# Joining a new token order for the QUADW quads, two DMAs for the rows of maxima, a changed first spread, and wide unused products

## The chip, the cores and the metric

The kernel runs on one core of one Trainium2 chip. A core has TensorE (PE), VectorE (DVE), ScalarE (ACT), GpSimd (POOL) and a queue for DMA issues (SP); PEld in the profile is TensorE's weight load, which runs beside the matmuls. The metric is the device time of one launch in microseconds, lower is better. Everything is fp32 at the boundary, and the kernel gets its precision from products of "high" and "low" halves (fp32r operands and their remainders).

## The reference

One block of a conditioned transformer, with S = 2048 tokens and D = 576 channels:

```
sa, ca, ga, sb, cb, gb = split(silu(c) @ w_mod, 6)
h = layernorm(x) * (1 + ca) + sa
q = h @ wq          # 32 heads of 18
k = h @ wk          # one head of 18, shared
v = h @ wv          # one head of 18, shared
o = softmax(q k^T / sqrt(18)) v      # per head
x = x + ga * (o @ wo)
h = layernorm(x) * (1 + cb) + sb
x = x + gb * (gelu(h @ w1 + b1) @ w2 + b2)      # w1: 576 x 4608
```

## The kernel before

The tokens are cut in four blocks `tb` of 512 (TB), and a block in four tiles of 128 (NT). The work goes through three phases.

**Phase 1, projections.** The modulation is computed, `x` is normalised (`ln1_stats`, `ln1_apply`), transposed by TensorE and spread by `h_evac` (L226): ACT forms the modulated fp32 value `hf`, then DVE (`first=True`) or ACT copies its high half into `zt`, and the engine `e` subtracts to form the low half (L233). The weights are split likewise by `split_wq` (L380: ACT copies, POOL subtracts at L384) and `split_rest` (L386: one DVE subtraction on the last chunk's upper half). For the first block, a loop runs the five `h_evac`s with the subtraction on DVE and with the high half copied by DVE for even k. `busy(n)` (L390) issues n matmuls of 128x128 on the identity whose product nobody reads. `q_chunk`, `k_block` and `v_block` are the projection products; q goes through DRAM (`qscr`) and comes back with `load_q` as `QST[n]`, a tile per quad. At the end of the last block (`i == 4`) a `busy(1)`, one `unit()` and another `busy(1)` are issued; `unit()` computes row maxima of scores.

**Phase 2, attention.** The 32 heads by 4 blocks are 32 quads of 4 heads and 512 tokens: quad n has `tb, qd = divmod(n, 8)`. The softmax's row maximum is found one quad ahead from extra score products, negated, and written into two spare rows (high and low half) of each half of `QST[n + 1]`, so that the score product of the next quad comes out with it subtracted. What runs when in a quad is a string of tokens written out by hand: QUAD for n = 0 to 8, QUADW for n = 9 to 30, LAST for n = 31. The strings give the program order on TensorE, and with it the order in which each other engine gets its part, since every engine executes in order:

- `S0`, `S1`: a score matmul 64x128 by 512 into `psB` (L932) and ACT's exponential of it into `P` (L934); 64 a quad. The digit names the row group (64 of 128 rows) of TensorE that is used.
- `M0`, `M1`: a maxima matmul into `psM` (L319) and DVE's reduction of it (L954), for the next quad. `X1`: a matmul with a difference of keys into `psB` (L942) and ACT's relu (L945); `R1`: a maxima matmul into `psM` and a DVE operation that joins it with the relu's result (L952).
- `Vj`: j units of probability times V (`pv_mm`, L922), four matmuls each, into `psC`, which lag eight units behind the scores; a quad has 64.
- `F1`, `F2`: `smax_fin1` reduces the maxima on DVE; `smax_fin2` (L357 to L365) transposes them on TensorE into a bank of `psB`, lets ACT copy the high half (L359) and DVE form the low half (L360), and has SP issue four DMAs into the rows of `QST[n + 1]` (L364).
- `T1`, `RC`, `T2`, `OS`: the steps of `post_quad` (L731) for the quad before: after ACT's evacuation of `psC` (L738), which is issued when the last V unit of that quad is, DVE transposes (L741); `RC` is DVE's reciprocal (L744) and POOL's scaling (L745); `T2` transposes back (L747); `OS` has ACT copy the high half (L757), POOL subtract (L758) and SP issue four DMAs into `ATT[tb]`. The tile `ATT[0]` is made by a generator of later steps (L551), the others here, ahead of `OS`.
- `WO`: one piece of the output projection (`wo_next`, L723 and L727), only in QUADW and LAST.

`psB` has four banks and `psM` three. After every fourth V unit, `between` runs a step or two of two background generators: `fill` (weights of later steps, normalisation of finished rows by `ln2_rows`, L585 among it) and `prep` (sums of MLP weights on POOL with their DMAs). Four units are one key chunk; `prep` pauses at three "quiet" chunks whose numbers are computed from where `F2` and `RC` stand in the string (`kf`, `kr`, L989). SP issues all DMAs.

**Phase 3, MLP.** The MLP runs over 36 half steps `v` with products of sums of blocks (a Strassen-like scheme): the first layer's products at L1147, the gelu at L1156 to L1168 on ACT, DVE and POOL, sums of its results at L1226 and around it, the second layer's products at L1250. Beforehand `form` (L1061) makes sums of the activations on POOL. The bias `b2` times the gate is needed in `ln2_rows` and in the last rows: `load_b2` loads it into a tile of the pool `px` in attention, `b2_scaled` (L631, L632) multiplies it by the gate and by 2 on POOL. At the start of the MLP `B2["b"] = load_b2()` loads it once more, and at `v == 0` `b2_scaled` multiplies it once more.

The old string of QUADW, whose tokens the prediction names:

```
M1 M1 S0 S0 X1 S1 M0 V4 S1 M0 S1 S0 M1 M0 V4 M0 S1 S0 M0 S1 T1 M0 X1 V4 S1 RC S0 S0 M1 M0 S1 V4
S0 R1 M1 S0 S1 M0 S1 V3 S1 M0 S0 X1 M0 M0 S1 V2 M0 S1 S0 R1 V2 M0 X1 M0 S1 S0 S1 M0 V4 S0 T2 R1
M0 S1 OS S0 M1 WO S0 R1 M1 S0 M1 S0 X1 V3 S0 M1 M0 S1 S1 M1 S0 V3 M0 S1 S0 R1 S0 M0 X1 V3 M0 S1
X1 M0 S1 M0 S1 V4 S1 M0 R1 S0 M1 S0 V4 S0 M1 M0 F1 S1 S0 S1 V4 M0 S1 M0 X1 S0 M1 F2 V4 M1 S0 S0
S1 M0 S1 M0 V3 R1 S0 S0 S1 R1 M0 V3 S0 S1 M0 S1 M0 S1 V3 M0 S1 M1 S0 M1 S0 V3
```

The last V unit of the quad before is the eighth, so its evacuation (L738) comes after the second group, `V4 ... V4`, of a string.

Of the kernel before, what the change touches and what calls it, by code (L numbers as in the profile page):

```python
# [8 lines left out]
F32 = mybir.dt.float32  # L9
F32R = mybir.dt.float32r  # L10
AF = mybir.ActivationFunctionType
ALU = mybir.AluOpType
# [20 lines left out]
def block_kernel(ctx: ExitStack, tc, x, wqkv, wo, w1, b1, w2, b2, c, wmod, ident_in, out):  # L33
# [19 lines left out]
    def psB(): return PS["t"].tile([128, 512], F32, name="psB", bufs=PS["b"])  # L53
# [3 lines left out]
    def big(): return per.tile([128, 10, 512], F32R, name="big", bufs=3)  # L57
# [297 lines left out]
    def smax_fin2(n):  # L355
        p = psB()
        pe.transpose(p[:16, :128], MR.pop(n), ident)  # L357
        ms = pa.tile([16, 2, 128], F32R, name="ms")
        ac.activation(ms[:, 0], p[:16, :128], AF.Copy, scale=-1.0)  # L359
        ve.scalar_tensor_tensor(ms[:, 1], p[:16, :128], -1.0, ms[:, 0].bitcast(F32), op0=ALU.mult, op1=ALU.subtract)  # L360
        for g in range(2):
            for s in range(2):
                r = 64 * g + R3 + s
                sy.dma_start(QST[n][r:r + 1].rearrange("o p (t c) -> o (p t) c", c=128).bitcast(F32),  # L364
                             ms[8 * g:8 * (g + 1), s].bitcast(F32))  # L365


    for t in range(NT):
# [12 lines left out]
    def split_wq(k, cs):  # L381
        ac.activation(wqh[:, k, cs], wqr[:, k, cs], AF.Copy)
        if k < KD - 1:
            po.tensor_tensor(wql[:, k, cs], wqr[:, k, cs], wqh[:, k, cs].bitcast(F32), op=ALU.subtract)  # L384

    def split_rest(cs):  # L386
        o = wqh[64:, KD - 1, cs]
        ve.tensor_tensor(o, wqr[64:, KD - 1, cs], o.bitcast(F32), op=ALU.subtract)

    def busy(n):  # L390

        p = psB()
        for _ in range(n):
            pe.matmul(p[:, :128], ident, ident, start=True, stop=True)

    busy(6)
    for t in range(NT):
# [9 lines left out]
        mod_sum(k)  # L407
    mod_cols(0, psB(), sel)
    mod_cols(1, psB(), unity[:, :1])
    busy(5)  # L410
    for k in range(KD):
        split_wq(k, slice(504, WQC))
    split_wq(0, slice(0, 504))
    split_rest(slice(504, WQC))
    for k in range(KD):
        h_evac(hp[k], zt, k, ve, k % 2 == 0)
    for k in range(1, KD):
        split_wq(k, slice(0, 504))
    split_rest(slice(0, 504))
    pick = p1.tile([128, 2, 128], F32R, name="pick")  # L420
    ones = p1.tile([128, 1], F32, name="ones")
    ve.memset(pick.bitcast(F32), 0.0)
# [23 lines left out]
    for tb in range(NB):  # L446
        nz = big() if tb + 1 < NB else None
        for i, m in enumerate((4, 0, 1, 2, 3)):
# [15 lines left out]
            if tb == NB - 1:  # L464
                if i == 0:
                    unit()
                elif i == 3:
                    smax_fin1(0)
                if i == 4:
                    busy(1)  # L470
                    unit()
                    busy(1)
            if nz is not None:
                for k in {1: (0, 1, 2), 2: (3, 4)}.get(i, ()) if tb else {3: (0, 1, 2), 4: (3, 4)}.get(i, ()):
                    h_chunk(tb + 1, nz, k)
# [147 lines left out]
        yield  # L623

    def load_b2():
        b2g = px.tile([128, D], F32, name="b2g")
        sy.dma_start(b2g, b2.to_broadcast([128, D]))
        return b2g

    def b2_scaled(b2g):  # L630
        po.tensor_mul(b2g, b2g, BC[:, 2, :])  # L631
        po.tensor_scalar(b2g, b2g, 2.0, None, op0=ALU.mult)  # L632
        return b2g
# [99 lines left out]
    def post_quad(n, PV):  # L733
# [13 lines left out]
        ve.transpose(O, T.rearrange("p a b -> p (a b)"))  # L747
        yield
        if tb not in ATT:
            assert tb  # L750
            ATT[tb] = big()
        A = ATT[tb].rearrange("p (s k) t -> p s k t", s=2)
        if n == NQT - 1:
            os = A[:, :, KD - 1, :]
# [126 lines left out]


    LAG = 8
    QUAD = """S0 M0 S1 S1 M0 V3 S0 M1 S1 M0 M1 S0 V3 M0 S1 M1 S0 V2 M0 S1 S1 M0 X1 S0 V4 T1 X1 M0 M1 M0 S1 S0
            V4 S1 RC M0 S1 S0 M0 S0 M1 V3 S0 M1 R1 S1 S0 M0 X1 V3 M0 S1 S1 R1 S0 M0 S1 V3 M0 X1 M0 S0 S1 S0
            M1 V3 M0 S1 S1 M0 S0 R1 S0 V3 R1 S0 S1 M1 S0 M0 X1 V3 M0 S1 M0 S1 S0 S0 R1 V3 M0 X1 S0 M1 S0 M1
            V3 S1 M0 M0 S1 T2 S0 S1 V4 M0 S1 S0 M1 S0 M1 V3 S0 R1 S1 M0 F1 S1 S0 V3 X1 M0 S1 M0 R1 S0 F2 OS
            V4 M0 M1 S0 S1 M0 X1 V4 S1 M0 S1 S0 M1 M0 S1 V2 R1 S0 M1 S0 V2 S0 S1 M0 M1 V2 S1""".split()
    QUADW = """M1 M1 S0 S0 X1 S1 M0 V4 S1 M0 S1 S0 M1 M0 V4 M0 S1 S0 M0 S1 T1 M0 X1 V4 S1 RC S0 S0 M1 M0 S1 V4
            S0 R1 M1 S0 S1 M0 S1 V3 S1 M0 S0 X1 M0 M0 S1 V2 M0 S1 S0 R1 V2 M0 X1 M0 S1 S0 S1 M0 V4 S0 T2 R1  # L890
            M0 S1 OS S0 M1 WO S0 R1 M1 S0 M1 S0 X1 V3 S0 M1 M0 S1 S1 M1 S0 V3 M0 S1 S0 R1 S0 M0 X1 V3 M0 S1
            X1 M0 S1 M0 S1 V4 S1 M0 R1 S0 M1 S0 V4 S0 M1 M0 F1 S1 S0 S1 V4 M0 S1 M0 X1 S0 M1 F2 V4 M1 S0 S0
            S1 M0 S1 M0 V3 R1 S0 S0 S1 R1 M0 V3 S0 S1 M0 S1 M0 S1 V3 M0 S1 M1 S0 M1 S0 V3""".split()
# [88 lines left out]
    for n in range(NQT):  # L982
# [3 lines left out]
        else:  # L986
            order = LAST
        if n < NQT - 1:
            kf, kr = (sum(int(tok[1]) for tok in order[:order.index(a)] if tok[0] == "V") // 4 for a in ("F2", "RC"))  # L989
            quiet = kf - 2, kf - 1, kr - 1  # L990
        for tok in order:
            if tok[0] == "V":
# [357 lines left out]
    for v in range(NV):  # L1350
# [158 lines left out]
```

## Time and profile before

| what | value |
|---|---|
| median of 3 runs | 2224.63 us |
| lowest and highest of them | 2224.18 and 2224.81 us |
| the profiled execution: its own time | 2227.88 us |
| the profiled execution: its span in the trace | 2225.8 us |
| first score matmul of attention | 130.8 us |
| evacuations of the quads' outputs (L738), first and last | 176.4 and 1375.9 us |
| the MLP | from about 1390 us to the end |
| scores' exponentials on ACT (L934) | 2013 of 620 ns |
| maxima's reductions on DVE (L954) | 1476 of 682 ns |
| memory traffic | 308.00 MB, mean 138 GB/s |

A line of the trace's order of time reads: start in us, duration in us, engine, line, operation, written tile <- read tiles, size, count; in brackets the idle time of the engine ahead of it and what ended it. A row that stands for several instructions has their count behind an x and their whole stretch as its duration. A row of the busy time by stretches has the window and its length, then busy us and count of instructions for PE, PEld, DVE, ACT and POOL, then the granted clock of TensorE (1.00 is full), the DMA engines' share, and GB/s. A row of one line's instructions has the shortest, median and longest duration in ns, and the first and last start. The bottom line of the page's chain gives the share of each engine in the work that ended last.

### The profile page before, as it was taken

How to read it: one execution, taken by the hardware profiler on the slowest of the kernel's cores; microseconds unless marked ns; L12 is line 12 of the kernel's file. 1: busy time of each engine (PE TensorE's matmuls, PEld its weight loads, DVE VectorE, ACT ScalarE, POOL GpSimd, SP SyncE). 2: the span in 40 equal slices, each digit the busy share in tenths (PEclk: the TensorE clock that was granted, in tenths of full speed). 3: DMA queues.
4: the chain of work that ended last, by engine and by line, in shares of the span. 5: the costliest groups of instructions: out<-in, count | busy, mean ns of one | idle time of the engine just before them, and what ended most of it. 6: DMA issues, size and time to landing. Idle time of an engine off the chain costs nothing.

```text
span 2225.8 us, 46116 instructions
## 1 busy us (share of the span) xinstructions
PE 2204.6 (99%) x16638; PEld 1450.8 (65%) x16638; DVE 1931.1 (87%) x3417; ACT 1639.8 (74%) x3145; POOL 1524.9 (69%) x1761
## 2 busy tenths in 40 slices
PE   8999999999999999999999999999999999999999
PEld 6654545454544545445454446888888898989898
DVE  7589999999999999999999983887888878888887
ACT  5569999999999999999999998544444444343443
POOL 6654356666776687677676640988888867877776
PEclk9999999999999999999999999999999999999999
DMA  6242143343333332333333322666666646676664
GB/s 228 85 133 93 34 128 122 127 137 109 125 121 123 115 129 94 114 130 111 115 121 118 125 70 69 200 179 174 178 179 181 185 129 182 180 218 188 177 184 124
DMA packets 184776, 308.00 MB, mean 138 GB/s; under 512 B 19711, under 2 KB 75407, under 8 KB 184549
## 3 DMA queue, kind: packets, MB, share of 16 engines
q1 hardware_dynamic: 184405, 304.91, 44.2%
q8 instruction: 132, 2.16, 0.4%
q14 instruction: 95, 0.78, 0.1%
q10 hardware_dynamic: 144, 0.15, 0.0%
HBM read 200.97 MB, written 93.79 MB: 132 GB/s over the span
## 4 chain that ended last, share of the span: by engine, by line
PE 92%; ACT 1%; DVE 1%; POOL 0%; issue 0%; DMA 0%; ACTq 0%; POOLq 0%; DVEq 0%
PE psC L922 23%; PE psB L1147 18%; PE psA L1250 16%; PE psB L932 14%; PE psM L319 12%; PE psB L723 2%; PE psB L942 2%; PE psA L1284 1%; ACT P L934 1%; PE psA L723 0%; PE psB L155 0%; PE psB L248 0%; PE psB L357 0%; DVE mx L344 0%; DVE mx L337 0%
## 5 line engine op out<-in xcount | busy, mean ns | idle before, releaser
L934 ACT ACTIVATE P<-psB 128x512 f32<-128x512 f32 x2013 | 1055.0, 620 | 42.7 <-PE psM L319 19.4
L954 DVE TENSOR_REDUCE mx<-psM 128x1 f32<-128x512 f32 x1476 | 934.2, 682 | 30.7 <-PE psM L319 16.0
L932 PE MATMUL psB<-qst,KS 64*128 64x512 f32 x2013 | 606.3, 434 | 0.1
L319 PE MATMUL psM<-KS,qst 64*128 64x512 f32 x1722 | 591.5, 435 | 0.6 <-DVE mx L337 0.5
L922 PE MATMUL psC<-P,V 128*32 128x256 f32 (+3 forms) x6608 | 569.0, 440 | 0.0
L932 PEld LDWEIGHTS psB<-qst,KS 64*128 64x128 f32 x2013 | 302.6, 184 | 218.3 <-ACT P L934 185.5
L319 PEld LDWEIGHTS psM<-KS,qst 64*128 64x128 f32 x1722 | 284.0, 184 | 186.1 <-DVE mx L954 130.5
L1147 PE MATMUL psB<-ops,w1a 128*128 128x512 f32 x1512 | 393.8, 396 | 0.2 <-DVE h L1162 0.2
L1147 PEld LDWEIGHTS psB<-ops,w1a 128*128 128x128 f32 x1512 | 270.1, 188 | 46.6 <-DVE h L1162 0.6
L922 PEld LDWEIGHTS psC<-P,V 128*32 128x32 f32 x6608 | 147.0, 108 | 187.9 <-issue 160.4
L1256 DVE TENSOR_TENSOR XT<-psA,XT 128x576 f32<-128x576 f32 x330 | 241.7, 753 | 20.1 <-PE psA L1250 14.7
L1250 PEld LDWEIGHTS psA<-w2s,big 128*128 128x128 f32 x1584 | 222.9, 188 | 15.5 <-POOL big L1224 3.6
L1250 PE MATMUL psA<-w2s,big 128*128 128x288 f32 x1584 | 230.8, 295 | 0.9 <-POOL big L1224 0.8
L1160 ACT ACTIVATE psB<-gs 128x512 f32<-128x512 f32 x144 | 86.7, 602 | 127.9 <-DVE gs L1159 127.8
L1224 POOL TENSOR_TENSOR big<-s,big 128x512 fp32r<-128x512 f32 x132 | 170.9, 1295 | 10.6
L952 DVE CUSTOM_DVE_ANT_0 xc<-psM,xc 128x512 f32<-128x512 f32 x246 | 166.3, 682 | 12.7 <-PE psB L932 4.5
L1156 ACT ACTIVATE h<-psB,b1t 128x512 f32<-128x512 f32 x144 | 97.9, 680 | 102.0 <-PE psB L1147 79.7
L945 ACT ACTIVATE xc<-psB 128x512 f32<-128x512 f32 x246 | 154.6, 628 | 4.2 <-PE psM L319 1.5
L758 POOL TENSOR_TENSOR os<-O,os 128x512 fp32r<-128x512 f32 x31 | 39.9, 1286 | 171.3 <-ACT os L757 171.3
L1159 DVE SCALAR_TENSOR_TENSOR gs<-psB,h 128x512 f32<-128x512 f32 x144 | 98.5, 684 | 38.5 <-ACT psB L1157 38.3
L792 POOL TENSOR_TENSOR r<-r,r 128x256 fp32r<-128x256 f32 (+1 forms) x162 | 121.8, 752 | 13.0
L1165 ACT ACTIVATE big<-h 128x512 fp32r<-128x512 f32 x39 | 24.7, 633 | 133.8 <-DVE h L1162 133.8
(212 smaller groups left out, 3325.2 us busy)
## 6 DMA issues: line engine op xcount, KB each, us to landing
w1a<-w1scr SPq DMA_DIRECT2D x252, 256.0 KB
w2s<-w2sum SPq DMA_DIRECT2D x132, 288.0 KB
w1scr<-r SPq DMA_DIRECT2D x126, 256.0 KB
w2s<-w2scr SPq DMA_DIRECT2D x76, 288.0 KB
w2scr<-r SPq DMA_DIRECT2D x72, 288.0 KB
w2sum<-r SPq DMA_DIRECT2D x72, 288.0 KB
qst<-qscr SPq DMA_DIRECT2D x192, 72.0 KB
w1a<-w2scr SPq DMA_DIRECT2D x33, 288.0 KB
```

The source lines that it names most:

```text
L319: pe.matmul(o, QST[n][64 * g:64 * g + 64, p, 128 * qt:128 * (qt + 1)], KS[64 * g:64 * g + 64, 512 * kb:512 * (kb + 1)], start=True, stop=True)
L792: po.tensor_tensor(o[:, n:2 * n], src, o[:, :n].bitcast(F32), op=ALU.subtract)
L922: pe.matmul(PVt[n][32 * j:32 * (j + 1), cs], V[:, kc, :], t[:, j, cs], start=(kc == 0 and h0 == 0), stop=(kc == 15), skip_group_check=True)
L932: pe.matmul(t, KS[64 * g:64 * g + 64, 128 * kc:128 * (kc + 1)], QST[n][64 * g:64 * g + 64, i, :], start=True, stop=True)
L934: ac.activation(P[n, kc][:, 2 * i + g, :], t, AF.Exp, scale=SCALE)
L945: ac.activation(XC[-1], t, AF.Relu)
L952: ve.tensor_tensor_reduce(c, t, c, 1.0, -3.0e38, ALU.add, ALU.max, o)
L954: ve.tensor_reduce(o, t, axis=AX.X, op=ALU.max)
L1147: pe.matmul(o, x, y, start=(first and i == 0), stop=(i == len(terms) - 1), skip_group_check=True)
L1224: po.tensor_tensor(unit(u, 1), x, unit(u, 0).bitcast(F32), op=ALU.subtract)
L1250: pe.matmul(p[:, i, :288], x[:, ts_], W2S[k][:, y], start=(bool(first) and q == 0), stop=(q == 2), skip_group_check=True)
L1256: ve.tensor_tensor(o, p[:, :, :288], o, op=ALU.add)
```

## The change

It has five parts. (1) QUADW gets a new order of the same tokens; QUAD is wrapped anew, with its tokens as they were. (2) `smax_fin2` writes the rows of maxima with two DMAs instead of four, each covering both row groups. (3) In the first block's spread, `split_rest` gets its engine as an argument and runs once on POOL, ahead of `split_wq(0, ...)`; two of the five subtractions of `h_evac` (k = 1 and 3) go to POOL, and the high halves are copied by DVE for all k but 1. (4) `dense(n, w, x)` is added, n matmuls of the full 512 columns whose product nobody reads; a `dense(1)` replaces one of five `busy` products in the first block, and `dense(5)` and `dense(4)` replace the two `busy(1)` around the last `unit()`. (5) The scaled `b2` lives in the pool `per` and is kept, so that its second load and its second scaling go. Beside this, `post_quad` steps the generator `fill` until `ATT[0]` is there where it is wanted earlier, and the position of `F2` and `RC` reads V counts of two digits.

```diff
-        for g in range(2):
-            for s in range(2):
-                r = 64 * g + R3 + s
-                sy.dma_start(QST[n][r:r + 1].rearrange("o p (t c) -> o (p t) c", c=128).bitcast(F32),
-                             ms[8 * g:8 * (g + 1), s].bitcast(F32))
+        for s in range(2):
+            r = R3 + s
+            sy.dma_start(QST[n][r:r + 65:64].rearrange("g p (t c) -> g (p t) c", c=128).bitcast(F32),
+                         ms[:, s].bitcast(F32))
...
-    def split_rest(cs):
+    def split_rest(cs, e):
         o = wqh[64:, KD - 1, cs]
-        ve.tensor_tensor(o, wqr[64:, KD - 1, cs], o.bitcast(F32), op=ALU.subtract)
+        e.tensor_tensor(o, wqr[64:, KD - 1, cs], o.bitcast(F32), op=ALU.subtract)
...
+    def dense(n, w, x):
+
+        p = psB()
+        for _ in range(n):
+            pe.matmul(p, w, x, start=True, stop=True)
...
-    busy(5)
+    busy(2)
+    dense(1, ident, XT[:, 0, :512])
+    busy(2)
     for k in range(KD):
         split_wq(k, slice(504, WQC))
+    split_rest(slice(504, WQC), po)
     split_wq(0, slice(0, 504))
-    split_rest(slice(504, WQC))
     for k in range(KD):
-        h_evac(hp[k], zt, k, ve, k % 2 == 0)
+        h_evac(hp[k], zt, k, po if k in (1, 3) else ve, k != 1)
     for k in range(1, KD):
         split_wq(k, slice(0, 504))
-    split_rest(slice(0, 504))
+    split_rest(slice(0, 504), ve)
...
                 if i == 4:
-                    busy(1)
+                    dense(5, wqh[:, 0, :128], KS[:, :512])
                     unit()
-                    busy(1)
+                    dense(4, wqh[:, 0, :128], KS[:, :512])
...
     def load_b2():
-        b2g = px.tile([128, D], F32, name="b2g")
+        b2g = per.tile([128, D], F32, name="b2g")
...
         if tb not in ATT:
-            assert tb
-            ATT[tb] = big()
+            while not tb and tb not in ATT:
+                step(fill)
+            if tb not in ATT:
+                ATT[tb] = big()
...
+    QUADW = """M1 X1 S0 S1 M0 S0 R1 V4 M0 S1 M0 X1 S1 M0 V4 S0 M1 M0 S1 S0 S1 M0 V4 S0 M1 S0 S1 M0 X1 M0 V4 S0 M1
+            M0 S1 S0 S1 M0 V3 R1 S0 S1 R1 S0 M0 T1 S1 V4 S0 S1 M0 M1 M0 S1 V2 X1 S0 S1 M0 V3 RC M0 S1 S0 M1 S0
+            M1 V3 S1 S0 M0 M1 S0 S1 V3 M0 S1 S1 M0 S0 T2 R1 WO X1 M0 M1 M0 X1 S0 S1 V3 R1 S0 S0 M1 S1 M1 S0 V4
+            S0 M1 X1 M0 S1 S0 V3 R1 M0 S1 S0 S1 M0 V4 M0 S1 S0 R1 S0 S1 M0 V4 X1 F1 M0 S1 M0 M1 S0 F2 V3 S1 M0
+            S1 M0 S0 R1 S0 V3 M1 S0 M1 S0 S1 M0 S1 V3 M1 S0 S1 M0 M0 S1 OS V3""".split()
...
-            kf, kr = (sum(int(tok[1]) for tok in order[:order.index(a)] if tok[0] == "V") // 4 for a in ("F2", "RC"))
+            kf, kr = (sum(int(tok[1:]) for tok in order[:order.index(a)] if tok[0] == "V") // 4 for a in ("F2", "RC"))
...
-    B2["b"] = load_b2()
...
-        if v == 0:
-            b2_scaled(B2["b"])
```

More of the change, by code (lines that the diff above doesn't have):

```diff
@@ L883, in block_kernel @@
     LAG = 8
[L884 to L893, printed above, removed]
+    QUAD = """S0 M0 S1 S1 M0 V3 S0 M1 S1 M0 M1 S0 V3 M0 S1 M1 S0 V2 M0 S1 S1 M0 X1 S0 V4 T1 X1 M0 M1 M0 S1 S0 V4
+            S1 RC M0 S1 S0 M0 S0 M1 V3 S0 M1 R1 S1 S0 M0 X1 V3 M0 S1 S1 R1 S0 M0 S1 V3 M0 X1 M0 S0 S1 S0 M1 V3
+            M0 S1 S1 M0 S0 R1 S0 V3 R1 S0 S1 M1 S0 M0 X1 V3 M0 S1 M0 S1 S0 S0 R1 V3 M0 X1 S0 M1 S0 M1 V3 S1 M0
+            M0 S1 T2 S0 S1 V4 M0 S1 S0 M1 S0 M1 V3 S0 R1 S1 M0 F1 S1 S0 V3 X1 M0 S1 M0 R1 S0 F2 OS V4 M0 M1 S0
+            S1 M0 X1 V4 S1 M0 S1 S0 M1 M0 S1 V2 R1 S0 M1 S0 V2 S0 S1 M0 M1 V2 S1""".split()
+    QUADW = """M1 X1 S0 S1 M0 S0 R1 V4 M0 S1 M0 X1 S1 M0 V4 S0 M1 M0 S1 S0 S1 M0 V4 S0 M1 S0 S1 M0 X1 M0 V4 S0 M1
[3 more added lines that the diff above has]
+            S1 M0 S0 R1 S0 V3 M1 S0 M1 S0 S1 M0 S1 V3 M1 S0 S1 M0 M0 S1 OS V3""".split()
     LAST = """S1 S0 S1 S0 V8 S1 S0 T1 S1 S0 RC S1 S0 WO S0 S1 S0 T2 S1 V5 S1 S0 S1 S0 S1 OS S0 V11 S0 S1 S0 S1 S0
```

## The prediction

> **What bounds the kernel now.** I read the page first (busy shares, then the chain that ended last), then the busy time by stretches, then one quad in the order of time.
>
> ```profile
> span 2225.8 us, 46116 instructions
> ...
> PE 2204.6 (99%) x16638; PEld 1450.8 (65%) x16638; DVE 1931.1 (87%) x3417; ACT 1639.8 (74%) x3145; POOL 1524.9 (69%) x1761
> ...
> PE 92%; ACT 1%; DVE 1%; POOL 0%; issue 0%; DMA 0%; ACTq 0%; POOLq 0%; DVEq 0%
> ```
>
> The chain is TensorE's for 92% of the span; no other engine has more than 1%. An edit pays where PE waits, and nowhere else. In the attention stage the others are close behind (columns: span, then PE, PEld, DVE, ACT and POOL busy, clock, DMA share, GB/s):
>
> ```profile
> 600.00:800.00 200.00, 200.00 (x1757) 98.91 (x1753) 191.93 (x378) 189.92 (x383) 143.40 (x197) 1.00 0.34 113
> ```
>
> DVE is busy 191.93 and ACT 189.92 of 200 us, so neither has more than 5% to spare. The evacuation of a quad's output (L738) happens once a quad and marks the period; here it stands for a stretch of QUAD quads and then for one of QUADW quads:
>
> ```profile
> L738 ACT ACTIVATE O<-psC x7: 614/622/630, 214.2 to 439.2; 128x512 f32<-128x512 f32 x7
> ...
> L738 ACT ACTIVATE O<-psC x20: 597/597/601, 515.7 to 1266.9; 128x512 f32<-128x512 f32 x20
> ```
>
> That is 225.0/6 = 37.5 us for a QUAD quad and 751.2/19 = 39.5 us for a QUADW quad, which also does an output piece. QUADW drives 22 quads, n = 9 to 30. Inside one of them, PE's weight loads show bursts of score and maxima matmuls (S, M, X, R tokens) divided by groups of PV matmuls (V):
>
> ```profile
> 592.26 0.18 PEld L932 LDWEIGHTS psB<-qst,KS 64*128 64x128 f32 x1 [0.84 <-ACT P L934]
> ...
> 594.16 0.18 PEld L319 LDWEIGHTS psM<-KS,qst 64*128 64x128 f32 x1 [0.84 <-DVE mx L954]
> ...
> 596.26 0.40 PEld L932 LDWEIGHTS psB<-qst,KS 64*128 64x128 f32 x3 [0.84 <-ACT P L934]
> ...
> 596.96 0.18 PEld L932 LDWEIGHTS psB<-qst,KS 64*128 64x128 f32 x1 [0.18 <-ACT xc L945]
> ...
> 598.39 0.18 PEld L932 LDWEIGHTS psB<-qst,KS 64*128 64x128 f32 x1 [0.84 <-ACT P L934]
> ...
> 621.58 0.09 PEld L357 LDWEIGHTS psB<-ident,mxf 128*16 128x16 f32 x1 [0.37 <-ACT P L934]
> ...
> 622.78 0.18 PEld L319 LDWEIGHTS psM<-KS,qst 64*128 64x128 f32 x1 [0.84 <-DVE mx L954]
> ...
> 623.55 0.18 PEld L932 LDWEIGHTS psB<-qst,KS 64*128 64x128 f32 x1 [0.24 <-DVE ms L360]
> 624.76 0.18 PEld L319 LDWEIGHTS psM<-KS,qst 64*128 64x128 f32 x1 [0.62 <-DVE mx L954]
> ...
> 626.56 0.19 PEld L932 LDWEIGHTS psB<-qst,KS 64*128 64x128 f32 x2 [0.41 <-ACT P L934]
> ...
> 628.24 0.29 PEld L932 LDWEIGHTS psB<-qst,KS 64*128 64x128 f32 x2
> ```
>
> A burst starts at each of these rows except 596.96, 621.58 and 623.55. The waits of 0.6 to 0.84 us at their heads are the PV group streaming, not a stall. Six tokens and V4 take 592.26 to 594.16 = 1.90 us, seven tokens and V4 594.16 to 596.26 = 2.10, six and V3 626.56 to 628.24 = 1.68. Tokens of row groups 0 and 1 run in pairs, so six are three rounds and seven are four: a round costs 0.20, a V unit 0.22, and each burst about 0.4 beside them.
>
> **The quads' order.** Counting QUADW by this rule, old and new both have 69 rounds, 64 V units, 19 PV groups, one output piece and one F2 transpose. The PE work is the same, so the new order can win only what the old one loses in real waits and lose only what it adds. The old one's: the burst at 596.26 (T1 and the output's evacuation just ahead, three scores in its first three tokens) takes 2.13 instead of 1.90, lost 0.23, seen at 596.96; the burst at 624.76 takes 1.80 instead of 1.68, lost 0.12. Other bursts lose a few hundredths: about 0.4 us a quad, at most 0.4 x 22 = 8.8 to gain. The new order spreads its scores behind that evacuation evenly (S0 M1 S0 S1 M0 X1 M0), so I give it the 0.23. What it adds:
>
> - F1 and F2 now stand in one burst, followed by V3 instead of V4, so the next burst comes 0.2 us sooner, while DVE's copy of F2's result comes later behind F1. That copy frees a bank: 623.55 shows a score already held by it. I estimate 0.2.
> - OS moves to the end, so ACT's copy of the output stands ahead of the next quad's first exponentials, and four ACT tokens are due at once there: 0.1.
>
> Net -0.4 + 0.3, about -0.1 a quad; with a little off for the T2 wait below I take -1.5 us for 22 quads. Bounds: -8.8 (no wait left) and +6.6 (0.3 more a quad, the largest waits of these rows, 0.23 to 0.24, with a margin).
>
> T2 on DVE needs POOL's scaling of T (L745), which needs RC:
>
> ```profile
> 636.96 0.23 DVE L744 RECIPROCAL R<-T 128x16 f32<-128x16 f32 x1
> ...
> 640.80 1.05 POOL L745 TENSOR_TENSOR T<-T,R 128x512 f32<-128x512 f32 x1
> ...
> 646.15 0.66 DVE L747 STREAM_TRANSPOSE O<-T 128x512 f32<-128x512 f32 x1
> ...
> L585 POOL TENSOR_SCALAR Z<-XT,mv,rs x8: 2288/2294/2302, 546.0 to 1099.7; 128x576 f32<-128x576 f32 x8
> ```
>
> Here POOL starts 3.6 us after R ends and ends 4.3 us before T2. In the new order RC stands at V 28 and T2 in the burst at V 34, two bursts of 1.68 and most of a third, 4 to 5 us instead of 9. POOL may then be 3 to 4 us late. It is that late only where a normalised tile (L585, 8 of them) lies in its queue, and the output piece follows T2 at once and covers DVE. Value 0 to 0.1 a quad. QUAD is only wrapped anew, with the same tokens, and the wait for a missing ATT tile in post_quad concerns block 0 alone, which QUADW never handles before its tile is there: both cost nothing.
>
> **The two DMAs.**
>
> ```profile
> 622.97 2.82 SPq L364 DMA_DIRECT2D qst<-ms  x4
> ...
> 630.19 0.18 PEld L932 LDWEIGHTS psB<-qst,KS 64*128 64x128 f32 x1
> ```
>
> Four issues start at 622.97 over 2.82 us; the next quad's first score is at 630.19, without a wait. Two issues of the same bytes end 1.4 us sooner. In the new order that score comes some 7 us behind F2 instead of 8.6, still later. Value 0; no row shows the landing, so the bounds are 0 and -1.4 once, where attention begins.
>
> **b2 kept.** At the start of the MLP the b2 load and its two POOL products go.
>
> ```profile
> 1393.23 4.77 POOL L1061 TENSOR_TENSOR ops<-yr,ops 128x1024 fp32r<-128x1024 f32 x2 [40.32 <-ACT ops L1059]
> 1397.95 1.43 POOL L631 TENSOR_TENSOR b2g<-b2g,BC 128x576 f32<-128x576 f32 x1
> ...
> 1401.10 0.61 POOL L1167 CAST gt<-h 128x512 fp32r<-128x512 f32 x1
> ...
> 1407.01 0.30 PEld L1250 LDWEIGHTS psA<-w2s,big 128*128 128x128 f32 x2 [0.59 <-POOL big L1223]
> ...
> 1408.35 1.36 PEld L1250 LDWEIGHTS psA<-w2s,big 128*128 128x128 f32 x10 [1.04 <-POOL big L1224]
> ```
>
> POOL runs without a pause from 1393.23 to the operand that PE waits for at 1407.01 and 1408.35. PE's idle time there is 1.04 and, of the 0.59, about 0.4: 1.45 us. POOL comes 1401.10 - 1397.95 = 3.15 us sooner, more than that wait; behind it PE is late next itself. -1.45, bounds -3.15 and 0.
>
> **The dense products.** The clock falls to half three times:
>
> ```profile
> 18.20:21.60 3.40, 2.57 (x23) 2.38 (x23) 2.14 (x4) 2.33 (x5) 2.50 (x5) 1.00 1.06 389
> 21.60:25.00 3.40, 3.40 (x8) 2.37 (x9) 3.33 (x7) 3.37 (x7) 0.08 (x1) 0.50 1.05 392
> ...
> 48.90:52.30 3.40, 3.40 (x11) 1.80 (x10) 2.31 (x3) 3.37 (x6) 0.62 (x1) 0.50 0.79 266
> ...
> 130.80:134.30 3.50, 2.85 (x12) 1.33 (x11) 3.50 (x5) 2.51 (x5) 0.22 (x1) 0.99 0.57 157
> 134.30:141.10 6.80, 6.80 (x30) 2.84 (x32) 4.66 (x9) 4.71 (x9) 0.00 (x0) 0.50 0.94 294
> ```
>
> Each fall follows a stretch in which PE does little. dense(5) and dense(4) stand ahead of the third, in place of two small products:
>
> ```profile
> 123.01 2.36 PE L248 MATMUL psB<-big,wA 128*126 128x512 f32 x9
> ...
> 129.75 0.73 PE L319 MATMUL psA<-KS,qst 64*128 64x512 f32 x3 [0.63 <-DVE mx L337]
> ...
> 130.83 0.50 PE L932 MATMUL psB<-qst,KS 64*128 64x512 f32 x1
> 131.57 0.50 PE L319 MATMUL psM<-KS,qst 64*128 64x512 f32 x1 [0.24 <-DVE mx L337]
> ```
>
> One such product costs 2.36/9 = 0.26, so five cost 1.3 and four 1.05. The five lie in the wait for DVE that ends at 129.75; the four push the first score by 0.7 (129.75 + 0.73 + 1.05 = 131.53 against 130.83), but the maxima matmul at 131.57 waits for DVE anyway: cost 0.1. If the clock holds, 6.8 us at half rate become 3.4, less some 1.4 us in which the maxima are paced by DVE: -2.0, net -1.9. Bounds: -3.4 and +2.3 (all nine uncovered, clock falls all the same). [...]
>
> **The first spread.** split_rest and two of five subtractions go to POOL, one copy from ACT to DVE.
>
> ```profile
> 42.65 1.30 POOL L233 TENSOR_TENSOR big<-hf,big 128x512 fp32r<-128x512 f32 x1
> ...
> 42.96 1.54 DVE L233 TENSOR_TENSOR big<-hf,big 128x512 fp32r<-128x512 f32 x1 [3.00 <-ACT big L232]
> ...
> 50.66 0.69 DVE L233 TENSOR_TENSOR big<-hf,big 128x512 fp32r<-128x512 f32 x1 [0.59 <-ACT big L232]
> ```
>
> POOL needs 1.30 for what DVE does in 0.69, and beside it DVE's own took 1.54. DVE sheds work, but POOL's weight subtractions, next in the path, start later. Value 0; bounds -1.7 (half of the 3.4 us at half clock) and +1.2 (two subtractions, 0.61 dearer each). [...]
>
> **Sum.** -1.5 - 1.45 - 1.9 = -4.85. The profiled execution took 2227.88 us (span 2225.8), 3.25 above the median 2224.63; I set the change against the median: 2219.8.
>
> **Rivals.**
>
> - Nothing gained in the quads and the clock falls all the same: only b2 counts, 2223.2. [...] Against it: the visible 0.23.
> - No wait left in the quads: -8.8 - 1.45 - 1.9 = -12.15, 2212.5. For it: even spacing in most bursts. Against it: the banks held behind F2.
> - T2 waits for POOL (slower). POOL's queue at RC holds what the quad's start put there; if it is over 4 us late, DVE stalls at T2 and PE behind it. At 0.5 us in each of 22 quads, +11: 2224.63 + 11 - 3.35 = 2232.3. For it: the 3.6 us seen. Against it: the tiles lie in 8 quads, and the piece covers.
> - The change may not do what it says: dense may leave the clock as it is; that is in the first rival.
>
> **Chances.** Forecast 0.45, nothing 0.25, no wait left 0.18, T2 0.12. A measurement tells about 0.2% (4.4 us) from no change. Of the forecast's 0.45, at its edge, 0.29 is faster: faster 0.47, same 0.16 + 0.25 = 0.41, slower 0.12. The range leaves out most of T2's case and the ends: 2212 to 2228.
>
> **What would show it.** L738 in QUADW quads: 39.4 us a period is the forecast, 39.1 no waits, over 39.7 T2. No wait of PE on POOL at the first L1250. Full clock behind the first score. It is wrong if PE's period changes by more than 0.4 us, or if attention starts over 1 us later.

## The result and the profile after

The changed kernel takes 2243.25 us (median of 5 runs, 2241.53 to 2246.1) against 2224.63 us before on the same chip: 18.6 us slower, a ratio of 1.0085 with a 95% interval of 1.0073 to 1.0096. The forecast was 2219.8 us, the range 2212 to 2228.

Three lines of the page of the changed kernel come first: the span, the busy times, and the engines' shares of the chain that ended last.

```profile
span 2240.0 us, 46391 instructions
...
PE 2209.6 (99%) x16819; PEld 1456.6 (65%) x16819; DVE 1930.9 (86%) x3415; ACT 1642.5 (73%) x3144; POOL 1527.3 (68%) x1762
...
PE 84%; DVE 4%; POOL 4%; ACT 1%; issue 1%; DMA 0%; SPq 0%; POOLq 0%; DVEq 0%; ACTq 0%
```

No engine has more work to speak of, but the chain left TensorE: its share fell from 92% to 84%, and DVE and POOL, which had 1% and 0%, have 4% each. Something now ends last that involves both. The same evacuations as in the prediction show where (the lines of the new file are some seven to nine further down: L738 is L745, T2's L747 is L754):

```profile
L745 ACT ACTIVATE O<-psC x20: 597/624/657, 511.0 to 1282.5; 128x512 f32<-128x512 f32 x20
```

Nineteen periods of QUADW took 771.5 us, 40.6 us each, where they were 39.5; "over 39.7" was the prediction's mark for the wait at T2. From the evacuation that precedes them to the last one it is 920.0 us (471.4 to 1391.5) against 899.4 (476.5 to 1375.9): 20.7 us lost in the quads, so some 2 us seem to be won elsewhere. The instructions of T2's line name the cause (below the durations stands how long the engine was idle ahead of it, and how often):

```profile
L754 DVE STREAM_TRANSPOSE O<-T x32: 698/702/712, 192.9 to 1393.9; 128x512 f32<-128x512 f32 x32
...
its engine sat idle before it (us, times) until:
  POOL T L752: 11.3, 5
```

In the kernel before, this list was empty:

```profile
L747 DVE STREAM_TRANSPOSE O<-T x32: 656/702/712, 197.6 to 1378.3; 128x512 f32<-128x512 f32 x32
...
its engine sat idle before it (us, times) until:
who waited for it (us, times):
```

Now DVE stands still at T2 for 11.3 us, in five quads, until POOL has scaled T (L752). The longest of these waits, in the order of time, on POOL, DVE and TensorE's weight loads:

```profile
549.91 2.31 POOL L592 TENSOR_SCALAR Z<-XT,mv,rs 128x576 f32<-128x576 f32 x1
...
557.26 1.95 POOL L135 MEMSET qst<- 32x1024 f32 x2
...
569.36 0.79 POOL L840 TENSOR_TENSOR w2b<-w2b 128x288 f32<-128x288 f32 x1
570.11 1.05 POOL L752 TENSOR_TENSOR T<-T,R 128x512 f32<-128x512 f32 x1
```

```profile
562.63 0.24 DVE L751 RECIPROCAL R<-T 128x16 f32<-128x16 f32 x1
...
566.56 1.24 DVE L963 TENSOR_REDUCE mx<-psM 128x1 f32<-128x512 f32 x2
571.19 0.71 DVE L754 STREAM_TRANSPOSE O<-T 128x512 f32<-128x512 f32 x1 [3.39 <-POOL T L752]
571.83 0.65 DVE L961 CUSTOM_DVE_ANT_0 xc<-psM,xc 128x512 f32<-128x512 f32 x1
```

```profile
572.54 0.18 PEld L319 LDWEIGHTS psM<-KS,qst 64*128 64x128 f32 x1 [3.57 <-DVE mx L961]
```

None of these POOL rows has a bracket: POOL went from the normalised tile at 549.91 through the background steps without a pause, and reached the scaling at 570.11, 7.24 us after R was ready (562.63 + 0.24 = 562.87). T2 was due at about 567.8 and started at 571.19. Behind it on DVE stood R1's operation (L961), which holds a bank of `psM`; the maxima matmul that needs that bank waited 3.57 us, and with it everything on TensorE. The output piece covered nothing: it is a VectorE addition and products, and it stands behind R1 like the M tokens of the same burst.

The wait has a second price. The busy time by stretches, around that wait (columns as before; PEclk is the value behind the five engines):

```profile
569.00:572.50 3.50, 0.41 (x3) 0.00 (x0) 1.31 (x4) 0.60 (x1) 3.34 (x7) 1.00 0.25 87
573.70:577.10 3.40, 3.40 (x27) 1.59 (x22) 2.62 (x6) 2.73 (x7) 3.28 (x3) 0.50 0.47 176
```

TensorE did 0.41 us of work in 3.5 us, and then ran 3.4 us at half rate (0.50). The same followed one other of the five waits, that of 2.73 us. By an estimate from these lengths, two such stretches cost about 2 x 1.7 = 3.4 us. The three early ones that the kernel before showed (at 21.6, 48.9 and 134.3 us) are missing in this execution; what that is worth, the experiments say.

The periods of the quads, from the starts of these evacuations, give the rest of the account (us; in all rows but the first the background work also puts layer-norm statistics on DVE):

| evacuations starting at (after) | before | after |
|---|---|---|
| 1204 to 1283, little but sums in the background | 39.24 to 39.27 | 39.10 to 39.18 |
| every second quad, seven from 595 to 1084, in which DVE also copies transposed rows (`yr<-psB`) | 39.86 to 39.93 | 40.34 to 40.41 |
| between them, no wait at T2: 717 and 962 | 39.27 to 39.29 | 39.47 to 39.49 |
| between them, waits at T2: 551, 636, 797, 881, 1042 | 39.25 to 39.29 | 44.43, 40.99, 43.78, 40.69, 42.23 |

Against the 39.48 us of their neighbours without a wait, the five quads of the last row are 14.7 us longer together, which is the 11.3 us of waiting and the 3.4 us of the clock. The other 6 us of the 20.7 have nothing to do with T2: they are the 0.2 to 0.5 us a quad that the middle rows show.

### The profile page after: what moved, and what is told of

It is laid out like the page before. It is cut to its first block, busy times and chain, and to the rows that moved or that the text cites. A ratio compares the mean times of both kernels' runs of the same rounds, so it can differ in the third digit from the quotient of the medians.

```text
span 2240.0 us, 46391 instructions
## 1 busy us (share of the span) xinstructions
PE 2209.6 (99%) x16819; PEld 1456.6 (65%) x16819; DVE 1930.9 (86%) x3415; ACT 1642.5 (73%) x3144; POOL 1527.3 (68%) x1762
## 3 DMA queue, kind: packets, MB, share of 16 engines
q8 instruction: 133, 2.18, 0.4%
## 4 chain that ended last, share of the span: by engine, by line
PE 84%; DVE 4%; POOL 4%; ACT 1%; issue 1%; DMA 0%; SPq 0%; POOLq 0%; DVEq 0%; ACTq 0%
PE psC L931 20%; PE psB L1155 18%; PE psA L1258 16%; PE psM L319 11%; PE psB L941 11%; DVE mx L963 2%; PE psB L730 2%; PE psB L951 2%; PE psA L1292 1%; DVE xc L961 1%; POOL r L801 1%; PE psA L730 1%; ACT P L943 1%; POOL Z L592 0%; POOL r L800 0%
## 5 line engine op out<-in xcount | busy, mean ns | idle before, releaser
L941 PE MATMUL psB<-qst,KS 64*128 64x512 f32 x2013 | 591.3, 432 | 0.4 <-ACT xc L954 0.2
L931 PE MATMUL psC<-P,V 128*32 128x384 f32 (+3 forms) x6784 | 569.6, 433 | 0.0
L941 PEld LDWEIGHTS psB<-qst,KS 64*128 64x128 f32 x2013 | 308.2, 184 | 174.7 <-ACT P L943 125.1
L319 PEld LDWEIGHTS psM<-KS,qst 64*128 64x128 f32 x1722 | 271.1, 184 | 208.7 <-DVE mx L963 151.6
L931 PEld LDWEIGHTS psC<-P,V 128*32 128x32 f32 x6784 | 152.9, 108 | 194.9 <-issue 166.8
L767 POOL TENSOR_TENSOR os<-O,os 128x512 fp32r<-128x512 f32 x31 | 39.9, 1286 | 230.4 <-ACT os L766 219.2
L961 DVE CUSTOM_DVE_ANT_0 xc<-psM,xc 128x512 f32<-128x512 f32 x246 | 166.0, 681 | 19.7 <-PE psM L319 12.1
```

The source lines that it names most:

```text
L319: pe.matmul(o, QST[n][64 * g:64 * g + 64, p, 128 * qt:128 * (qt + 1)], KS[64 * g:64 * g + 64, 512 * kb:512 * (kb + 1)], start=True, stop=True)
L931: pe.matmul(PVt[n][32 * j:32 * (j + 1), cs], V[:, kc, :], t[:, j, cs], start=(kc == 0 and h0 == 0), stop=(kc == 15), skip_group_check=True)
L941: pe.matmul(t, KS[64 * g:64 * g + 64, 128 * kc:128 * (kc + 1)], QST[n][64 * g:64 * g + 64, i, :], start=True, stop=True)
L961: ve.tensor_tensor_reduce(c, t, c, 1.0, -3.0e38, ALU.add, ALU.max, o)
```

## The experiments

The theory after the traces was: the order alone costs the time, because T2 came closer to RC, POOL is not done with the scaling by then, and DVE stops. Rivals: the other parts carry some of the loss; DVE or POOL are overfull at that place whatever the distance; the gain that the first stage showed in the trace was real and hides a larger loss. Each run stands against the kernel before on the same chip (medians there 2224.0 to 2224.65).

**The order, without and alone.** The first kernel has the old QUADW in the changed file, the second the new QUADW in the file of before.

```diff
-    QUADW = """M1 X1 S0 S1 M0 S0 R1 V4 ...
+    QUADW = """M1 M1 S0 S0 X1 S1 M0 V4 ...
```

> The change with QUADW's old order put back; the rest of it stays. Theory (the order alone costs the time, because T2 on VectorE waits for GpSimd's scaling of T): attention still starts some 5 us earlier than in the kernel before (output evacuations of quad 0 at 171.7 instead of 176.4 us), the QUADW periods return to 39.26 and 39.9 us, no wait of VectorE at T2, and the b2 part stays: 2224.6 - 4.7 - 1.4 = 2218.5 us, 2216 to 2221. Rival (some of the loss comes from the other parts, by the moved DMAs, SP's queue or the kept b2): 2222 us or more.

Measured: 2224.4 us against 2224.0, ratio 1.0 (0.9992 to 1.0009). The quads are back at 39.26 and 39.9 us with no wait at T2, but the gain that the theory kept for the start did not appear in the median, so the 2216 to 2221 us were missed. The other four parts together neither gain nor lose, within the interval; what each does is told below.

> The kernel before with nothing but the new QUADW. Theory: the whole loss of the quads is here, + 20.7 us by the two traces, so 2245 us (2241 to 2249), with five or six quads in which VectorE stands 1 to 3.5 us at T2 for GpSimd. Rival (the order costs only together with the two DMAs or the kept tile): under 2235 us. The start of attention should stand as in the kernel before, 176 us for the first evacuation; if it comes at 172 to 174 us, the gain of the first stage was a matter of one execution and not of the change.

Measured: 2246.33 us, ratio 1.0098 (1.0084 to 1.0112), as the theory has it: waits at T2 of 3.43, 1.38, 2.73 and 2.65 us, and two of 0.3. Its first stage is that of the kernel before, and it tells what the comparison of two executions had hidden: the first evacuation starts at 172.6 us here, not at 176.4, with the same instructions. One wait of TensorE in the projections, from two executions of the same code, that of before and that of this kernel:

```profile
48.02 1.89 PEld L248 LDWEIGHTS psB<-big,wA 128*128 128x128 f32 x7 [2.90 <-ACT qs L279]
```

```profile
46.04 1.46 PEld L248 LDWEIGHTS psB<-big,wA 128*128 128x128 f32 x7 [1.40 <-ACT qs L279]
```

ACT waits there for a DMA that carries q to DRAM (`qscr<-qs`) to land, 2.18 us in the first of these executions and 0.69 in the second, so the landing differs by execution. Over the twelve traces TensorE's wait is 0.6 to 2.9 us, the longest in that of before; in that of the changed kernel it is 0.6. Against the 172.6 us of the second execution, 3.8 of the 4.7 us by which attention seemed to start earlier (171.7 against 176.4) are a matter of the execution and not of the change; the profiled execution of before lay 3.25 us above its median.

**Three ways to take the wait away.** They leave all work in. The first puts T2 later, the second leaves the tokens alone and moves POOL's background sums behind T2, the third puts RC earlier.

```diff
-... M0 S1 S1 M0 S0 T2 R1 WO ... S0 M1 X1 M0 S1 S0 V3
+... M0 S1 S1 M0 S0 R1 WO ... S0 M1 T2 X1 M0 S1 S0 V3
```

> The changed kernel with T2 moved from V 34 to V 41 of QUADW, so that it stands some 10 us behind RC, as in the old order; RC and everything else stay. Theory (T2 waits for the scaling): VectorE's waits at T2, 11.3 us in five quads, go, and the two half-rate stretches of 3.4 us that follow the longest two go with them (3.4 us): 2243.25 - 11.3 - 3.4 = 2228.5 us (2226 to 2232). Rival (VectorE or GpSimd are simply overfull at that place, and the wait moves to the next instruction that needs GpSimd): over 2238 us.

Measured: 2232.44 us, ratio 1.0036 (1.0023 to 1.0049). No wait at T2 is left, and no fall of the clock in the quads. But it is 4 us over the expected 2228.5: T2's 0.70 us on DVE now come into the burst at V 41, and the next one, at V 44, took 2.19 us instead of 1.89; so every quad pays 0.3.

```diff
+            early, late = ((kr - 3, kr - 2), (kr + 1, kr + 2)) if n > NQ else ((), ())
...
-        if n > 3 and kc not in quiet:
-            for _ in range(1 + (kc % 4 != 3)):
+        if n > 3 and kc not in quiet and kc not in early:
+            for _ in range((1 + (kc % 4 != 3)) * (1 + (kc in late))):
                 step(prep)
```

> The changed kernel with QUADW's order as it is; in quads 9 to 30 the background steps of GpSimd's weight sums that stood two and three chunks ahead of RC's chunk are issued behind T2 instead, the same number of them. Theory (what GpSimd has queued ahead of the scaling makes T2 wait): GpSimd has some 5 us less queued at RC, and of the five waits at T2, 1.1 to 3.4 us, at most small rests are left: 2243.25 - 11 - 3.4 = 2229 us, up to 2234. Rival (the wait is that of the short distance on VectorE itself, or GpSimd is overfull wherever the steps stand): 2238 us or more.

Measured: 2227.82 us, ratio 1.0018 (1.0009 to 1.0027). This is the cleanest of the three: in the quads, DVE and ACT have the changed kernel's instructions in the same order, and on POOL the scaling alone changes its place among the others. R and the scaling of the quad shown above, and the line of T2:

```profile
563.62 0.24 DVE L751 RECIPROCAL R<-T 128x16 f32<-128x16 f32 x1
...
564.97 1.42 POOL L838 TENSOR_TENSOR w2b<-w2b,BC 128x576 f32<-128x576 f32 x1
566.34 1.05 POOL L752 TENSOR_TENSOR T<-T,R 128x512 f32<-128x512 f32 x1
567.71 0.23 POOL L149 TENSOR_SCALAR rs<-mv 128x1 f32<-128x1 f32 x1 [0.32 <-DVE mv L148]
```

```profile
L754 DVE STREAM_TRANSPOSE O<-T x32: 698/701/711, 194.3 to 1379.9; 128x512 f32<-128x512 f32 x32
...
its engine sat idle before it (us, times) until:
who waited for it (us, times):
```

The scaling starts 2.48 us behind R (566.34 - 563.86) instead of 7.24, nothing stands under the idle time, and 15.4 us of the 18.6 are gone. What POOL had queued ahead of the scaling was the cause, and moving the queue alone removes it.

```diff
-... T1 S1 V4 S0 S1 M0 M1 M0 S1 V2 X1 S0 S1 M0 V3 RC M0 S1 ...
+... T1 S1 V4 RC S0 S1 M0 M1 M0 S1 V2 X1 S0 S1 M0 V3 M0 S1 ...
```

> The changed kernel with RC moved from V 28 to V 23 of QUADW, T2 and all else in place; the pause of the background sums moves with RC. RC comes 2.9 us earlier, and four of GpSimd's background steps, some 4 us, are no longer queued ahead of the scaling. Theory (T2 waits for what GpSimd has queued ahead of the scaling): all five waits at T2 (3.4 us the longest) go, and with them the clock's falls: 2243.25 - 11.3 - 3.4 = 2228.5 us, 2226 to 2232. Rival (the number of queued steps does not matter, only a fixed distance in V units): T2 is 11 V units behind RC then, not 6, and waits of 1 us or more remain in the quads with a normalised tile: 2233 us or more.

Measured: 2234.36 us, ratio 1.0044 (1.003 to 1.0058). All five waits are gone, so the rival of a fixed distance falls, though its time (2233 us or more) was met; the least margin between the scaling and T2 is 0.91 us. The time is again above the expected, and the quads with the least background work take 39.36 us instead of 39.12. The excess lies in the bursts behind the reciprocal's new place, V 25 (1.63 us instead of 1.45) and V 28 (1.79 instead of 1.72), so its 0.24 us on DVE probably came into a fuller stretch; no run tests this alone.

**What is left of the order.** With the wait gone by moved sums, the periods are 39.5 and 40.4 us where they were 39.27 and 39.9 before. By the starts of the bursts, three of them are longer in some of the quads with statistics than in those with the least background work: V 28 in the one half of the quads (2.07 us against 1.71), V 52 and V 61 in the other (2.16 against 1.88, 2.25 against 1.78). One more kernel moved the statistics a chunk earlier.

```diff
-        if kc % 2 and (held[0] != "T" or not pieces):
+        if (kc + (n > NQ)) % 2 and (held[0] != "T" or not pieces):
```

> The kernel with the background sums moved behind T2, and in quads 9 to 30 the steps of the other background work (finished rows' statistics on VectorE among them) called after even key chunks instead of odd ones, so one chunk earlier. Theory (the 0.2 to 0.5 us a quad that are left of the loss come from the two statistics of 0.45 us, which fall into the bursts with RC, F1 and OS): the bursts at V 28, V 52 and V 61 return to 1.72, 1.89 and 1.78 us from 2.07, 2.17 and 2.25, and the periods change by some tenths, to 39.1 to 39.3 and 39.7 to 40.0 if the new places have room: 2227.8 - 5 = 2223 us; 2220 to 2228. Rival (the excess belongs to the new tokens themselves): these bursts keep their times, 2227 to 2229 us.

Measured: 2229.94 us, ratio 1.0027 (1.0017 to 1.0037). Bursts, in us, medians over six or seven quads:

| burst | moved sums | and statistics a chunk earlier |
|---|---|---|
| V 25 | 1.45 | 1.73 |
| V 28 (RC) | 2.07 | 1.79 |
| V 31 | 1.68 | 2.10 |
| V 52 (F1, F2) | 2.16 | 2.20 |
| V 61 (OS) | 2.25 | 1.78 |

The excess leaves two of the three bursts and turns up in others, at or behind the ones where the statistics (0.45 us each on DVE) now fall, so it belongs to them and not to the tokens. The expected time was missed: the new places had no more room than the old ones. That V 52 kept its excess fits as well: in the trace, one statistic moved from the burst at V 48 to that at V 44, and the other (L147) from V 58, ahead of the excess at V 61, to V 52 itself.

**The start.** One kernel takes the first spread back, with the five small unused products ahead of it, and one the dense products; both have QUADW's old order.

```diff
+    split_rest(slice(504, WQC), ve)
-        h_evac(hp[k], zt, k, po if k in (1, 3) else ve, k != 1)
+        h_evac(hp[k], zt, k, ve, k % 2 == 0)
```

> QUADW's old order, and the first spread as in the kernel before (split_rest and all five subtractions on VectorE, five small unused products); the dense products, the two DMAs and the kept b2 stay. Theory (the new spread costs 1.0 us, because GpSimd's weight subtractions start later and TensorE waits for them): from the first projection product to the first key product 8.8 us instead of the 9.82 of the changed kernel, whatever the clock, and 2224.4 - 1 = 2223.4 us. Rival (the new spread is worth its trouble, because it removes a clock fall at 20 to 25 us): the stretch stays at 9.8 us or more, 2225 us or more.

Measured: 2222.31 us, ratio 0.9992 (0.9983 to 1.0001). The stretch from the first projection product to the first key product is 29.69 - 20.89 = 8.80 us, against 9.83 with the new spread. The waits that make it, first of the kernel with the new spread (the one with the old order), then of this one:

```profile
23.17 0.53 PEld L248 LDWEIGHTS psB<-big,wA 128*128 128x128 f32 x3 [0.61 <-POOL big L233]
...
25.99 2.62 PEld L248 LDWEIGHTS psB<-big,wA 128*128 128x128 f32 x12 [1.27 <-POOL big L233]
29.37 0.52 PEld L248 LDWEIGHTS psB<-big,wA 128*126 128x126 f32 x3 [0.76 <-POOL wA L383]
```

```profile
21.56 2.99 PEld L248 LDWEIGHTS psB<-big,wA 128*128 128x128 f32 x12 [0.38 <-DVE big L233]
25.05 1.92 PEld L248 LDWEIGHTS psB<-big,wA 128*128 128x128 f32 x9 [0.50 <-DVE big L233]
27.85 0.52 PEld L248 LDWEIGHTS psB<-big,wA 128*126 128x126 f32 x3 [0.88 <-POOL wA L383]
```

The two subtractions on POOL make TensorE wait 0.61 and 1.27 us. That costs 0.5 to 1.0 us: five executions with the old spread took 8.8 to 9.3 us for this stretch, all seven with the new one 9.81 to 9.83, also the one of them that had a half-rate stretch there. Four of the five with the old spread ran at half rate for 3.4 or 6.8 us at this place and the fifth, which did not, took 9.2 us, so the length of this stretch does not follow the clock.

By the durations, DVE and POOL also held each other up here: POOL's first subtraction took 1.75 us, where one of the same size took 1.30 in the prediction's row at 42.65, and two operations on DVE took about 1 us longer than in the old spread. The rows of the new spread (the kernel with the old order) come first, then those of the same copy and the same subtraction on DVE in the old spread:

```profile
21.37 1.75 POOL L233 TENSOR_TENSOR big<-hf,big 128x512 fp32r<-128x512 f32 x1 [0.40 <-ACT big L232]
24.55 1.39 POOL L233 TENSOR_TENSOR big<-hf,big 128x512 fp32r<-128x512 f32 x1 [1.43 <-DVE big L230]
...
21.99 1.42 DVE L230 CAST big<-hf 128x512 fp32r<-128x512 f32 x1
...
24.84 1.65 DVE L233 TENSOR_TENSOR big<-hf,big 128x512 fp32r<-128x512 f32 x1
```

```profile
22.02 0.42 DVE L230 CAST big<-hf 128x512 fp32r<-128x512 f32 x1
...
24.30 0.69 DVE L233 TENSOR_TENSOR big<-hf,big 128x512 fp32r<-128x512 f32 x1
```

Beside POOL's first subtraction a copy on DVE took 1.42 us instead of 0.42. POOL's second subtraction then waited 1.43 us for DVE's next copy, and beside it DVE's last subtraction took 1.65 us instead of 0.69. The one wide unused product that the new spread has ahead of it was not measured by itself.

```diff
-                    dense(5, wqh[:, 0, :128], KS[:, :512])
+                    busy(1)
                     unit()
-                    dense(4, wqh[:, 0, :128], KS[:, :512])
+                    busy(1)
```

> QUADW's old order, and the two small unused products in place of dense(5) and dense(4); all else as changed. Theory (the dense products keep the clock up at the start of attention and cost 0.7 us of a later first score): the clock falls to half for 3.4 to 6.8 us between 127 and 142 us; from the transposition of the first maxima to the first output evacuation 50.8 to 51.3 us instead of 49.5; 2224.4 + 1.5 = 2225.9 us. Rival (the fall was a matter of one execution): no fall there, 48.8 us for this stretch, 2223.7 us.

Measured: 2225.32 us, ratio 1.0005 (0.9996 to 1.0015). Without the dense products, and with them (the kernel of the old order), by stretches:

```profile
127.00:130.40 3.40, 2.62 (x11) 1.31 (x9) 2.80 (x4) 1.19 (x3) 1.28 (x1) 1.00 0.37 122
130.40:137.20 6.80, 6.69 (x24) 3.49 (x28) 6.52 (x11) 5.78 (x11) 0.00 (x0) 0.50 0.79 225
```

```profile
127.20:130.60 3.40, 3.40 (x15) 1.68 (x14) 2.80 (x3) 0.93 (x3) 1.29 (x1) 1.00 0.25 87
130.60:134.00 3.40, 2.59 (x12) 1.04 (x11) 3.40 (x7) 3.40 (x7) 0.00 (x0) 1.00 0.72 214
```

The theory of the dense products holds in size, with one limit. All three executions without them fell to half rate for 6.8 us there; of nine with them, six did not fall and three fell for 3.4 us. From the transposition of the first maxima to the first evacuation it is 50.5 to 51.2 us without, 49.2 to 49.5 with them and no fall, 50.2 to 50.6 with a fall. In the medians the two cannot be told apart (ratios to the kernel before of 1.0005 without them and 1.0 with them).

**Can the wait that the prediction saw be won back?** The prediction's gain in the quads was the burst at 596.26, 0.2 us longer than others like it. Two kernels (old order and old spread) rearranged it, so that its scores stand further apart.

```diff
-... T1 M0 X1 V4 S1 RC S0 S0 M1 M0 S1 V4
+... T1 M0 X1 V4 M1 S0 RC S1 M0 S0 S1 V4
```

> The old order with the old spread, the dense products, the two DMAs and the kept b2, and in QUADW one burst rearranged: S1 RC S0 S0 M1 M0 S1 behind the output's evacuation becomes M1 S0 RC S1 M0 S0 S1, so that its scores stand 2nd, 3rd, 5th and 6th among the tokens and not 1st, 2nd, 3rd and 6th. Theory (the 0.2 us that this burst is longer than others of six tokens and V4 is a wait for a bank that ScalarE holds while it evacuates the output, and can be won back): the burst takes 1.90 us instead of 2.11, 22 x 0.2 = 4.4 us: 2222.3 - 4.4 = 2218 us, the period 39.05 us. Rival (ScalarE or VectorE is full around it, so that the wait comes back in the bursts behind): the period stays at 39.27 us, 2222 us or more.

> As the other rearranged burst, but S1 RC M0 S0 M1 S0 S1: scores stand 1st, 3rd, 5th and 6th. Theory: the first score's bank is free in time, since the wait was seen at the second and third; 1.90 to 1.95 us for the burst, 2218 to 2219 us. Rival: the wait comes back in the bursts behind, period 39.27 us, 2222 us or more.

Measured: 2223.54 us, ratio 0.9995 (0.9986 to 1.0004), and 2222.7 us, 0.9992 (0.9983 to 1.0001), where 2218 was expected. The burst kept its 2.1 us, the period its 39.26. ACT in the second of them, around the output's evacuation (L743):

```profile
666.72 2.09 ACT L941 ACTIVATE P<-psB 128x512 f32<-128x512 f32 x4
668.75 0.60 ACT L743 ACTIVATE O<-psC 128x512 f32<-128x512 f32 x1
669.25 1.57 ACT L941 ACTIVATE P<-psB 128x512 f32<-128x512 f32 x3
670.68 0.63 ACT L952 ACTIVATE xc<-psB 128x512 f32<-128x512 f32 x1
671.21 4.17 ACT L941 ACTIVATE P<-psB 128x512 f32<-128x512 f32 x8
```

ACT has no pause for over 8 us around that wait. The reading is that the burst's scores wait for banks which ACT leaves only when it has worked off what lies before, and that the order of the scores in the burst changes nothing in that. Both runs fit it; none gives ACT less to do there.

No version is clearly faster than the kernel before. The best, the old order and the old spread with the dense products, the two DMAs and the kept b2, stands at 2222.31 us, 2.3 us below; its interval reaches 1.0001.

## Why the prediction was wrong, step by step

- **T2 behind RC: this is the step that failed.** The prediction saw the distance fall from 9 us to 4 or 5 (it was 4.9 in the quad shown), saw that POOL could be 3 to 4 us late, and still put 0 to 0.1 us on it, for two reasons. "It is that late only where a normalised tile ... lies in its queue" is true of the five waits, which all fall in quads with such a tile (five of the eight). But it took the lateness of the old place, 3.6 us in the quad shown and 4.15 at most, for that of the new one. RC stands 16 V units later there, so other background steps lie ahead of the scaling, and it came up to 7.24 us after R, with only 4.9 us to T2. And "the output piece follows T2 at once and covers DVE" left out R1 between them, whose bank TensorE needs at once. Measured: 11.3 us of waiting, 3.4 us of half rate behind it, and 15.4 us by the kernel that only moved the sums.
- **The bound of that term.** The end of +6.6 us for the quads came from waits of 0.24 us at other places, not from the queue of the engine for which the new wait would be. The rival had the mechanism, with 0.12 as its chance. That its 0.5 us in each of 22 quads is also the mean measured (11.3 / 22 = 0.51) is luck, since five quads had it all; its 2232.3 us lacked the clock's part and the statistics below.
- **The count of what is gained in the quads.** The forecast of -0.1 us a quad was measured at -0.13 where the background has little to do (39.26 to 39.13), and the equal counts of rounds were right. But its sum does not follow from its own terms: it grants the new order 0.23 us and then subtracts 0.4, and 0.23 against the 0.3 that is added would have been a loss of 0.07. That the size came out is partly luck. By the bursts' lengths in these quads, the burst at V 12 still takes 2.1 us (2.14 us where it was 2.12) but holds seven tokens instead of six, so one round of 0.2 now fits into what was a wait. OS costs 0.1 as forecast (V 61, 1.78 us against 1.68 for six tokens and V3). F1 and F2 in one burst cost the forecast 0.2 (1.88 against 1.68), but the old F2's burst already lost as much (2.10 against 1.90), which the prediction did not count.
- **The background's own steps on DVE** were left out, a term that the prediction put at nothing, though its window from 600 to 800 us had DVE at 96%. Where statistics fall on DVE the quads lose 0.2 to 0.5 us. By the kernel with moved sums this is about 5 us (904.5 us for the stretch of quads against 899.4).
- **The two DMAs:** 0, as forecast. SP issues them in 1.70 us instead of 3.26 ahead of the first score, and the first score comes 5.64 us behind the transposition without the dense products, 5.68 before.
- **b2 kept:** forecast -1.45. From the last evacuation to the end it is 849.9 us before and 850.1 with the order alone. In the kernels that keep b2 it is 848.4 to 848.6 with the new order, so -1.5 to -1.7, and 848.9 to 849.4 with the old one, so -0.5 to -1.0. No wait for POOL is left at the first product of the second layer.
- **The dense products:** forecast -1.9, measured -1.0 to -2.1 between the transposition and the first evacuation when the clock holds, and about -0.5 when it falls all the same, which happened in 3 of 9. The price was 0.7 us and not 0.1: the first score comes 6.4 us behind the transposition instead of 5.7, and no later wait swallows that; the measured gain has it in already. What sets these three apart from the six without a fall, no run shows.
- **The first spread:** forecast 0, bounds -1.7 and +1.2; measured +0.5 to +1.0, by POOL's subtractions being late. The upper bound counts POOL's 0.61 a subtraction and nothing for DVE, but DVE's last subtraction took 1.65 us beside POOL's instead of 0.69, much like the 1.54 in the prediction's row at 42.96. What TensorE waits for is POOL's two results, 0.61 and 1.27 us, the second of them late by DVE's copies too. The fall of the clock on which the bound of -1.7 counts cost nothing, since the stretch takes as long without it (9.2 us, against 8.8 to 9.3 with it).
- **What was set against the median.** The stretches at half rate in the profiled execution of before were taken as the median's. That execution was 3.25 us slower than the median, with a wait at 48 us that was 1.5 us longer than in the other trace of the same first stage. Its fall at 48.9 us is in none of the other eleven traces. A gain read from it was partly no gain.

## What to carry to other kernels

When two dependent steps on one engine are moved closer together with a step on another engine between them, price the other engine's queue at the new place, counting every background instruction that stands ahead there, and ask which bank the next instruction behind the waiting one holds. In this stage, where DVE is busy for 96%, half a microsecond found no free place: T2's 0.70 us cost 0.3 in a new burst, the reciprocal's 0.24 us cost about as much as it takes, and the statistics of 0.45 us cost 0.2 to 0.5 a quad where the new order met them. Before a short wait of TensorE is counted as a gain, look whether the engine it waits for has a pause around it; here ACT had none for 8 us, and two rearrangements of the burst won nothing.

## What the runs showed of the hardware

- Some of the waits at T2 within the quads were followed by half rate on TensorE (a granted clock of 0.50): 3.4 us of it after the waits of 3.39 and 2.73 us in the changed kernel, and 6.8 and 3.4 us after those of 3.43 and 2.65 in the kernel with the order alone. TensorE itself stood still for 2.4 to 3.2 us each time. The waits of 1.1 to 1.4 us were not followed by it, and neither were the 2.65 us of the changed kernel and the 2.73 of the other one, so in these runs the length alone didn't decide.
- With nine unused full-width products around the last `unit()` (five in 1.33 us and four in 1.20 us in the changed kernel's trace), TensorE kept full rate at the start of attention in six of nine executions and fell to 0.50 for 3.4 us in three; without them it fell for 6.8 us in all three.
- A wait of TensorE in the first stage that hangs on the landing of a DMA took 0.6 to 2.9 us from trace to trace, and 2.90 and 1.40 us in two executions of the same code; this spread is more than any of the small parts of the change is worth.
- In the new first spread, two DVE operations beside POOL's subtractions of 128x512 took longer than in the old one: a copy 1.42 us instead of 0.42, and a subtraction 1.65 us instead of 0.69.
